# Attention and two MLPs on one core: the reciprocal sums spread over partitions by TensorE instead of through DRAM

## The chip, the cores and the metric

The kernel runs on one core of a Trainium2 chip. The metric is the device time of one execution in microseconds (us). Beside the runs there is one profiled execution, from which every duration here comes. Engines are named as in the profile: PE is TensorE's matmul, PEld its weight load, DVE VectorE, ACT ScalarE, POOL GpSimd, SP SyncE, on whose queue all DMAs are issued.

## The reference

Attention over 4 batches, 8 heads, 576 positions and 64 dimensions a head, in which only scores within tau of the row's maximum count; then two MLPs on the 2304 tokens of width 512.

```python
scores = (q @ k.T) / sqrt(64)
scores = where(scores >= max(scores) - tau, scores, -1e9)
attn = exp(scores - max(scores))
attn = attn / (sum(attn) + 1e-9)
x = (attn @ v)                            # heads side by side: [2304, 512]
h = x @ w_in                              # [2304, 2048]
P = a0 + a1*h + a2*h**2 + a3*h**3
Q = 1 + abs(b0)*abs(h) + abs(b1)*h**2
x = (P / (Q + 1e-6)) @ w_out              # [2304, 512]
out = ((x @ w1) * (x @ w2)) @ w3 @ w_out2 # [2304, 512]
```

## The kernel before

Attention is worked per batch b (4), head pair c (4) and part u: u = 0 takes queries 0 to 255, u = 1 queries 256 to 511 together with the 64 queries that are left, the tail (u = 2 in `pv`), in which both heads of the pair share one block of 128 rows. For each block of 128 queries and each head, `qk` puts 576 scores a row into PSUM (tile S), `top` takes the maximum on DVE, `thr` the threshold, and `exp` the exponentials p and their row sum, one column of a small tile with queries on the partitions. p is split into an f16 part and its remainder (`p_hi`, `p_lo`, tile hl), turned by a DMA transpose (`p_t`, tiles pT and pL), and multiplied with the values, which are split likewise (vh, vl): `pv` makes 28 products of the form 64 head dimensions x queries, alternating between the two heads, whose results take partitions 0 to 63 and 64 to 127 of one PSUM bank (tag h, two banks).

The result has the queries along the columns, while the sums lie one query to a partition. `recip` (lines 551 to 559) adds 1e-9, inverts, transposes the tile in 32 x 32 blocks on DVE (sT) and writes it to DRAM (d_r). `spread` reads it back with each head's row repeated on 64 partitions (tile R). `x_split` and `x_tail` multiply the products in PSUM with R and split the outcome into two f16 parts, the input x of the first MLP (tiles xp, xl).

The MLPs work on 128 tokens (n, 18 of them): `h_product` (line 815), a rational function on ACT, DVE and POOL (tiles U, A, r, gg), a DMA transpose (`turn`, gg into gt), `y_product` (879); then `ab_product` (986), their product, another transpose, and `o_product` (1015). The weights arrive as 64-bit floats, are converted by three integer operations on DVE (`conv_w`, lines 683 to 689), scaled and split into two f16 parts (`split_w`), all in the first third.

Nothing is scheduled at run time. All steps are collected as numbered events; the string ORDER lists them, one token a step, with the letter of the engine for elementwise steps (v DVE, a ACT, p POOL) and the slots of the buffers that it takes. The program issues them in that order, and each engine works through its own part of it in order, waiting on semaphores. Helpers (`copy`, `rest`, `tt`, `small`) issue on the engine of the letter, so one line of theirs (330 to 353) stands for many steps.

Of the kernel before, what the change touches and what calls it, by code (L numbers as in the profile page):

```python
# [36 lines left out]
123a 43.7 16 43 127v.1 125.7 125a 156.1.0 43 16 30.1 140.1 129p 72.0 140 53.1 154p 159.0 161
134v.0 163v.1 136v 165.8 53 32.8 138 167.7 39.9 32 165a 39 167a 77.0.0 32 74.10 62.1 39 53 74
169a.0 59.2 79 171p 53 79p 173.0 74 79p 182.1.0 64.11 81.0 80.0 64 106.1 184.1 186 80 64 188a.2
190.8 61.12 116.1 55v.13 190a 61 175v.5 192.2 61 192a 219.1.0 83v.2.2 99.2 200a.0 207.0 177p 131  # L40
66.1 194p.3 221.2 83 207 202v 76.0 223 66 196v 101.14 198 225v.0 101 227.7 66 101 230.2 227a 209.1
112.2 230a 66 232p.8 142.0 78.15 118.16 78 244.1.0 118 78 118 85.0 80 234v 103.1 246.3 238p.1 80
248 240v 250a.1 252.3 215.4.6 82a.17 87.18 252a 107.0 114.19 87 255.7 114 257a.2 87 107 255a 114
89.0 68v.20 217p 598.2 269.1 70.0 93.1 105.21 269 259v 105 263a.3 283.1.0 281 105 93 91.22 623.1
285.0 287 107 91 288a.2 601.23 91 107 601 618.0 265v 601 290.7 93 626.24 143.2 290v 626 93 626
604.1 95a.25 620.26 620 620 97.1 144.1 128.0 57.0 179.1 146 146v 590.1 146p 242.2 590 130.27
109v.28 271.0 130 590 204 292.5 145.29 606.30 145 130 590 267 145 292v 147.1 148.0 609.0 606 120.2
277.1.0 606 151.1 609 294v.3 296p 609 299v.7 150a.3.3 301p 609 150 135.0 305.1.0 611a.31 122.32
593v.33 279p 596.0 307.1 122 308 122 153.34 166.2 124.0 310v.0 153 314.5 126.0 628.1 153 110.0
137.35 132.0 158.1 137 314a 137 321a.6 174.0 628 168.36 323p 168 312.5 133 628 168 312a 205.2  # L50
139.0 141 628 327.0 631a.37 176.38 160.39 176 160 176 160 189.0 178.0 149 328.2 354 316a.4 181.1
155.1 149 330a.1 206.40 157.1 318v 162.1 206 164 614.1 206 170.1 191.41 197.2 191 172 180 191 180
212.0 193.1 183.42 183 183 199.43 220.1 185.0 199 187.0 199 211.1 214.44 235.2 201.0 214 214 228.0
195 203 222.45 236.0 216.1 213 222 208.0 218.1 213v 210 222 303.1 237.46 224.1 210 213p 634.0 226
237 237 278.1 350.5.8 229.47 239.0 229 84.1 229 636 261 231.1 332.7 233 241 332v 356.1.0 291.2 241
304.0 325 339.0 352a 280.48 243 280 243 339 358.3 247a.49 245v.0 360 334a.2 273.0 272v.50 253a.51
361p.2 268v.52 251a.53 280 424.0 336p 371.1 424 253.0 297.0 275 264p.54 256a.55 249a.56 266a.1 424
274a.0 275a 424 253a 264.1 275v 306.10 260a.12 424 341.1 254a.11 247.0 258v.15 264a 306 363.7
251.1 306 247a 373.14 365.6 284.0 256.0 251v 262a.18 373 319 249.1 270a.21 373 256a 363a 260.0
311.1 249a 365a 378.1.0 286.22 260a 286 372a.3 286 367a.4 266.1 380.0 374p 317.0 381 254.0 266a  # L60
369v 383p.0 385.0 272.1 313.19 370.2 293.16 387.6 313 254a 293 385a 444.1 313 387a 293 331.1 426.0
272a 320.23 324.2 394a.7 320 338.4 320 426 396p 322.1 337.0 274.0 428.0 333.30 258.1 430 274v
400.1 430 270.0 258v 443 401.1 444 270v 403a.1 405.6 326.6 333 262.1 276a.4 326 446.1 333 268.0
446.0 326 351.1 428.1 448 357.2 268a 340.2 428.0 448 262a 347.1.0 433v 405a 340 446.1 412.1 435
340 445.0.1 412 435 349 376.0 353.3 437.0 461.1 353 344.0 414.0 447.2 349p 343.0 349v 461 437 398
345.0 437 345a 508.0 449 345p 463.0 437p 451a.2 466 453.1 508 439.0 353 309.1 359.26 315.1 407v.2
# [1177 lines left out]
```

## Time and profile before

| | us |
|---|---|
| median of 3 runs | 1139.39 |
| lowest and highest | 1138.14, 1145.7 |
| profiled execution, its own time | 1143.35 |
| its span | 1141.6 |
| PE busy in it | 1003.3 |
| DVE busy | 867.7 |
| ACT busy | 594.2 |
| POOL busy | 370.9 |

The span runs from the first instruction to the last of the profiled execution; 1.75 us of its own time lie around it. Busy time counts each engine by itself, so the engines overlap, and a share over the span is a mean over stages that are limited by different things. Mean durations of matmuls include their passage through the array, and neighbours overlap; what one costs in a stream is read from the chain, where a stretch of so many is given with its length.

### The profile page before, as it was taken

The numbers are of one execution on the slowest core, as the hardware profiler recorded it, in microseconds if no ns is written. First come the engines' busy times: TensorE is split into PE (matmuls) and PEld (weight loads), VectorE is DVE, ScalarE is ACT, GpSimd is POOL, SyncE is SP. The second block draws the span as 40 slices with busy tenths as digits, with TensorE's granted clock in tenths as the row PEclk, the third lists the DMA queues.
The fourth block names the chain that finished last, engine by engine and source line by source line (L and its number), as shares of the span: only waits on it lengthen the run. The fifth ranks groups of instructions, "written<-read, shape, count | busy, mean of one in ns | idle before, by whom it ended". The sixth has DMA issues, their size and how long they took to land.

```text
span 1141.6 us, 15703 instructions
## 1 busy us (share of the span) xinstructions
PE 1003.3 (88%) x5284; PEld 475.8 (42%) x5284; DVE 867.7 (76%) x1682; ACT 594.2 (52%) x1086; POOL 370.9 (32%) x377
## 2 busy tenths in 40 slices
PE   2779578388879898989899999899999998999998
PEld 1334233143334443444344444454444444444443
DVE  5886879888876699888798877988787765676552
ACT  4341566775554484747356545767755434352410
POOL 1220121561234234244434343643423322421211
PEclk9999779599999999999899999999999999999999
DMA  7978697766673958778675879795566446723223
GB/s 224 244 211 190 219 210 191 182 112 175 166 175 106 161 109 153 156 139 165 114 136 107 163 139 165 134 152 128 125 130 111 104 85 94 117 53 68 53 56 83
DMA packets 345088, 159.90 MB, mean 140 GB/s; under 512 B 313776, under 2 KB 321968, under 8 KB 345008
## 3 DMA queue, kind: packets, MB, share of 16 engines
q1 hardware_dynamic: 345008, 158.91, 66.7%
q8 instruction: 41, 0.67, 0.3%
q14 instruction: 39, 0.32, 0.1%
HBM read 74.71 MB, written 8.65 MB: 73 GB/s over the span
## 4 chain that ended last, share of the span: by engine, by line
PE 45%; DVE 17%; DMA 10%; issue 4%; ACT 4%; POOL 2%; SPq 2%; DVEq 0%; ACTq 0%; POOLq 0%
PE y L879 9%; PE h L815 9%; PE h L986 6%; PE y L1015 6%; PE S L986 5%; DMA gt<-gg 3%; PE h L601 3%; PE S L504 3%; DVE m L513 2%; DMA pT<-hl 2%; PE y L739 2%; DMA raw<-in_q_dram 2%; DMA R<-d_r 1%; PE S L499 1%; DVE U L835 1%
## 5 line engine op out<-in xcount | busy, mean ns | idle before, releaser
L879 PE MATMUL y<-wp,gt 128*128 128x512 f16 x864 | 200.5, 382 | 9.2 <-DMA gt<-gg 8.1
L815 PE MATMUL h<-wp,xp 128*128 128x512 f16 x768 | 180.4, 383 | 8.5 <-ACT wp L330 2.2
L346 POOL TENSOR_TENSOR hl<-p,hl 128x576 f16<-128x576 f32 x76 | 107.7, 1419 | 167.3 <-ACT hl L330 69.3
L504 PE MATMUL S<-raw 64*128 64x288 f32 x512 | 104.2, 472 | 50.2 <-DVE p L539 20.1
L986 PE MATMUL h<-wp,yy 128*128 128x512 f16 x576 | 137.6, 385 | 6.3 <-DVE U L837 3.1
L879 PEld LDWEIGHTS <-gt 128*128 128x128 f16 x864 | 83.4, 98 | 116.5 <-DMA gt<-gg 11.3
L513 DVE TENSOR_REDUCE m<-S 128x1 f32<-128x576 f32 x144 | 104.3, 748 | 28.0 <-PE S L504 19.5
L815 PEld LDWEIGHTS <-xp 128*128 128x128 f16 x768 | 74.0, 99 | 103.3 <-issue 21.0
L1015 PE MATMUL y<-wp,gt 128*128 128x512 f16 x432 | 103.4, 387 | 7.7 <-DMA gt<-gg 6.6
L346 POOL TENSOR_TENSOR gg<-A,r 128x512 f16<-128x512 f32 x46 | 60.8, 1323 | 137.6 <-DVE A L858 93.2
L536 ACT ACTIVATE S<-S,th 128x576 f32<-128x576 f32 x101 | 70.4, 709 | 63.3 <-DVE th L353 42.8
L823 ACT ACTIVATE U<-h,cf 128x512 f32<-128x512 f32 x72 | 55.8, 776 | 83.9 <-PE h L815 43.2
L986 PEld LDWEIGHTS <-yy 128*128 128x128 f16 x624 | 60.3, 99 | 90.2 <-issue 22.0
L504 PEld LDWEIGHTS S<-raw 64*128 64x128 f32 x512 | 56.7, 204 | 93.8 <-issue 26.1
L346 POOL TENSOR_TENSOR A<-A,r 128x512 f32<-128x512 f32 x41 | 54.1, 1321 | 108.9 <-ACT r L830 102.2
L835 DVE SCALAR_TENSOR_TENSOR U<-h,cf,U 128x512 f32<-128x512 f32 x72 | 53.5, 744 | 42.7 <-ACT r L830 18.9
L541 ACT ACTIVATE p<-S,xy 128x576 f32<-128x576 f32 x101 | 74.7, 742 | 10.4 <-DMA pL<-hl 6.3
L845 ACT ACTIVATE r<-A,lnb 128x512 f32<-128x512 f32 x72 | 52.0, 722 | 45.2 <-POOL A L346 27.1
L854 DVE SCALAR_TENSOR_TENSOR gg<-U,cf,r 128x512 f16<-128x512 f32 x72 | 58.3, 812 | 19.4 <-ACT r L847 16.1
L739 PE MATMUL y<-cw,dg 128*128 128x512 f32 x112 | 62.1, 636 | 11.6 <-DVE wp L334 6.2
L1015 PEld LDWEIGHTS <-gt 128*128 128x128 f16 x432 | 41.9, 100 | 61.2 <-DMA gt<-gg 8.4
L936 PE MATMUL h<-cw 128*128 128x512 f32 x128 | 62.3, 638 | 5.4 <-DVE cw L334 3.6
(195 smaller groups left out, 1672.9 us busy)
## 6 DMA issues: line engine op xcount, KB each, us to landing
rw<-in_moe_w_dram SPq DMA_DIRECT2D x32, 512.0 KB
rw<-in_moe_w_out_dram SPq DMA_DIRECT2D x24, 512.0 KB
raw<-in_k_dram SPq DMA_DIRECT2D x32, 288.0 KB
wr<-in_v_dram SPq DMA_DIRECT2D x16, 576.0 KB
rw<-in_moe_w_in_dram SPq DMA_DIRECT2D x16, 512.0 KB
wr<-in_v_dram SPq DMA_DIRECT2D x16, 320.0 KB
R<-d_r SPq DMA_DIRECT2D x32, 128.0 KB
out_dram<-A SPq DMA_DIRECT2D x16, 256.0 KB
```

What stands on the lines that cost most here:

```text
L346: (nc.gpsimd if eng[0] == "p" else nc.vector).tensor_tensor(o, x, y, op=op)
L504: nc.tensor.matmul(t[s][:, half, :HS], x[r, o:o + 128], y[r, keys], start=True, stop=True)
L513: nc.vector.tensor_reduce(st["m", b, c, blk][:, s:s + 1], t[:, :, :HS], axis=AX.XY, op=ALU.max, negate=True)
L536: nc.scalar.activation(t, t, AF.Prelu, bias=th, alpha=BIG)
L541: nc.scalar.activation(x, t, AF.Exp, bias=xy[:, 0:1], accum_out=su)
L739: nc.tensor.matmul(y, st["dg", dg], r, start=True, stop=False)
L815: nc.tensor.matmul(t, x[:, y, c, o:o + 128], w[:, a, :], start=c + i == 0, stop=c == KD - 1 and i == 2)
L835: stt(u, h, cf[:, 4:5], u, ALU.mult, ALU.mult)
L879: nc.tensor.matmul(st["y", n], x[:, 4 * a + j, :], w[:, y, :], start=f + j + i == 0, stop=f == 3 and j == 3 and i == 2)
L936: nc.tensor.matmul(t, st["cw", ("w3", m, j // 4)][:, o:o + 128], st["cw", ("wo2", j)], start=j == 0, stop=j == 7)
L986: nc.tensor.matmul(t, x[:, 4 * y + c, :], w[:, a, :], start=c + i == 0, stop=c == KD - 1 and i == 2)
L1015: nc.tensor.matmul(st["o", n], x[:, 4 * a + j, :], w[:, y, :], start=hf + j + i == 0, stop=hf == 1 and j == 3 and i == 2)
```

## The change

The reciprocal sums no longer go through DRAM. `recip` writes each reciprocal, times 1024, as an f16 value and an f16 remainder (tile rr). `spread` multiplies on PE: the stationary operand is one column of rr repeated 64 times, the moving one a diagonal tile (spot) with 2^-10 on it, so that column q of the result holds the reciprocal of query q on all 64 partitions; value and remainder add up in PSUM. It uses the upper half of the h bank whose lower half then takes `pv`'s products, and its second step copies the result into R on ACT or DVE. A full spread is 8 products, a tail spread (u = 2, which is now a step of its own) 4. The sums lie in tiles of five columns from a pool of three. ORDER is a new table for the new list of events: its tokens are renumbered, and steps change their places and, for 551 steps, their engine.

```diff
 ORDER = """
...
@@ -305,7 +308,7 @@
     BUFS = dict(
         w=57, gg=2, gt=3, xp=2, x4=4, dg=2, wr=3, U=2, A=2, r=2, G=9, pT=3, vh=4, vl=4,
-        R=2, m=4, th=3, sT=2, vs=2, sc=4, cf=6, xl=1,
+        R=2, m=4, th=3, su=3, rr=3, vs=2, sc=4, cf=6, xl=1,
     )
     places = []
@@ -363,7 +366,6 @@
         events.append((fn, args, *stream))
-    d_r = [dr.tile([32 * 128], F32, name=f"d_r{j}") for j in range(2 * B * NP)]
     d_y = [dr.tile([128, 1024], F16, name=f"d_y{n}") for n in range(NT)]
@@ -380,7 +382,7 @@
     lnb = cst.tile([128, 1], F32, name="lnb")
     c3 = cst.tile([128, 3], F32, name="c3")
     onesh = cst.tile([128, 128], BF16, name="onesh")
-    sums = [cst.tile([128, 32], F32, name=f"sums{j}") for j in range(3)]
+    spot = cst.tile([128, 128], F16, name="spot")
     qp = cst.tile([128, 128], F32, name="qp")
     wsc = cst.tile([128, 8], F32, name="wsc")
     acc = cst.tile([128, 56], F32, name="acc")
@@ -396,8 +398,9 @@
         nc.sync.dma_start(out=bb, in_=cb.rearrange("(o c) -> o c", o=1).to_broadcast([128, 2]))
         nc.gpsimd.memset(unit, 1.0)
         nc.gpsimd.memset(onesh, 1.0)
-        for t in sums:
-            nc.gpsimd.memset(t, 0.0)
+        nc.gpsimd.memset(spot, 0.0)
+        nc.gpsimd.affine_select(out=spot, in_=spot, compare_op=ALU.not_equal, fill=2.0**-10,
+                                base=0, pattern=[[-1, 128]], channel_multiplier=1)
         nc.vector.tensor_scalar(flag, tau_t, 0.0, 0.125, op0=ALU.is_ge, op1=ALU.mult)
@@ -525,9 +528,9 @@
         u = min(blk // 2, 1)
         if (u, s) == (0, 0) and blk == 0 or (blk, s) == (2, 0):
-            st["su", b, c, u] = sums[(2 * (NP * b + c) + u) % 3]
+            st["su", b, c, u] = T("su", [128, 5])
         p = T("G", [128, S], name="p")
-        x, k = p.rearrange("p (j c) -> p j c", j=2), 2 * s + blk - 2 * u if blk < 4 else 4
+        x, k = p.rearrange("p (j c) -> p j c", j=2), 2 * (blk - 2 * u) + s
         su, th = st["su", b, c, u][:, k:k + 1], st["th", b, c, blk][:, s:s + 1]
         t, m = st["S", b, c, blk][s][:, :, :HS], st["m", b, c, blk][:, s:s + 1]
         if by_dve(b, c, blk):
@@ -550,23 +553,30 @@
     def recip(b, c, u):
         n = 5 if u else 4
-        su, d = st["su", b, c, u], d_r[2 * (NP * b + c) + u]
-        nc.vector.tensor_scalar(su[:, :n], su[:, :n], 1e-9, None, op0=ALU.add)
-        nc.vector.reciprocal(su[:, :n], su[:, :n])
-        t = T("sT", [128, 32])
-        nc.vector.transpose(t, su)
-        yield
-        nc.sync.dma_start(out=d.rearrange("(k i q) -> i k q", i=4, q=32), in_=t)
+        su = st.pop(("su", b, c, u))[:, :n]
+        nc.vector.tensor_scalar(su, su, 1e-9, None, op0=ALU.add)
+        nc.vector.reciprocal(su, su)
+        t = st["rr", b, c, u] = T("rr", [128, 2, 5], F16)
+        nc.vector.tensor_scalar(t[:, 0, :n], su, 1024.0, None, op0=ALU.mult)
+        stt(t[:, 1, :n], su, 1024.0, t[:, 0, :n], ALU.mult, ALU.subtract)
     def spread(b, c, u):
-        d = d_r[2 * (NP * b + c) + u]
-        r = st["R", b, c, u] = T("R", [128, 320])
-        t = d[0:512].rearrange("(h o q) -> h o q", h=2, o=1)
-        nc.sync.dma_start(out=r[:, 0:256], in_=t.to_broadcast([2, 64, 256]))
-        if u:
-            t = d[512:640].rearrange("(h o q) -> h o q", h=2, o=1)
-            nc.sync.dma_start(out=r[:, 256:320], in_=t.to_broadcast([2, 64, 64]))
+        t, r = P("h", [128, 512]), st["rr", b, c, min(u, 1)]
+        st["pv", b, c, u] = t
+        for i in range(2 if u < 2 else 1):
+            for a in range(2):
+                for h in range(2):
+                    o, k = slice(64 * h, 64 * h + 64), slice(0, 128)
+                    w, d = r[:, a, 2 * i + h:2 * i + h + 1], t[o, 256 + 128 * i:384 + 128 * i]
+                    if u == 2:
+                        k, w, d = o, r[o, a, 4:5], t[o, 64:128]
+                    nc.tensor.matmul(d, w.to_broadcast([k.stop - k.start, 64]), spot[k, k],
+                                     start=a == 0, stop=a == 1)
+        yield
+        n = 256 if u < 2 else 64
+        y = st["R", b, c, u] = T("R", [128, n])
+        copy(y, t[:, n:2 * n])
     def p_hi(b, c, blk, s):
         hl = T("G", [128, 2 * S], F16, name="hl")
@@ -591,7 +601,7 @@
         n = 256 if u < 2 else 64
         if u < 2 and c == 0:
             st["xp", b, u] = T("xp", [128, 2, KD, TG], F16)
-        t = P("h", [128, 512])
+        t = st["pv", b, c, u]
         vh, vl = st["v", b, c]
         for j in range(14):
             for s in range(2):
@@ -603,12 +613,10 @@
                                  start=j == 0, stop=j == 13)
         for s in range(2 if u < 2 else 1):
             st.pop(("pT", b, c, u, s))
-        st["pv", b, c, u] = t
     def x_split(b, c, u):
-        t, r = st.pop(("pv", b, c, u)), st["R", b, c, u]
-        y, p = r[:, :256], st["xp", b, u]
+        t, y, p = st.pop(("pv", b, c, u)), st.pop(("R", b, c, u)), st["xp", b, u]
         nc.vector.tensor_tensor(y, t[:, :256], y, op=ALU.mult)
         yield
         copy(p[:, 0, c, :], y)
@@ -619,10 +627,10 @@
     def x_tail(b, c):
-        t, r = st.pop(("pv", b, c, 2)), st["R", b, c, 1]
+        t, y = st.pop(("pv", b, c, 2)), st.pop(("R", b, c, 2))
         if b % 2 == 0 and c == 0:
             st["xl", b // 2] = T("xl", [128, 2, KD, 128], F16)
-        y, p = r[:, 256:320], st["xl", b // 2][:, :, c, 64 * (b % 2):64 * (b % 2) + 64]
+        p = st["xl", b // 2][:, :, c, 64 * (b % 2):64 * (b % 2) + 64]
         nc.vector.tensor_tensor(y, t[:, :64], y, op=ALU.mult)
         yield
         copy(p[:, 0], y)
@@ -648,10 +656,11 @@
                 at(p_lo, b, c, blk, s)
                 at(p_t, b, c, blk, s)
         at(recip, b, c, u)
-        at(spread, b, c, u)
         if u:
+            at(spread, b, c, 2)
             at(pv, b, c, 2)
             at(x_tail, b, c)
+        at(spread, b, c, u)
         at(pv, b, c, u)
         at(x_split, b, c, u)
```

The order table is not legible as such; the rows that follow are each engine's instructions in program order. First SP at the last head pair of the last batch (b = 3, c = 3, u = 1): before,

```order
L586 DMA_TRANSPOSE pT<-hl 128x9x128 x4
L867 DMA_TRANSPOSE gt<-gg 128x8x128
L559 DMA d_r_97<-sT 4x32x32
L586 DMA_TRANSPOSE pT<-hl 128x9x128
L586 DMA_TRANSPOSE pL<-hl 128x9x128
L566 DMA R<-d_r_97 128x1x256
L569 DMA R<-d_r_97 128x1x64
L586 DMA_TRANSPOSE pL<-hl 128x9x128
L867 DMA_TRANSPOSE gt<-gg 128x8x128 x2
```

and with the change, at the same place:

```order
L596 DMA_TRANSPOSE pT<-hl 128x9x128
L1036 DMA out_dram<-A 128x512
L596 DMA_TRANSPOSE pT<-hl 128x9x128 x2
L596 DMA_TRANSPOSE pL<-hl 128x9x128
L596 DMA_TRANSPOSE pT<-hl 128x9x128 x3
L596 DMA_TRANSPOSE pL<-hl 128x9x128
L876 DMA_TRANSPOSE gt<-gg 128x8x128 x4
```

The write of sT to d_r and the two reads into R are gone from between the transposes of P (pT, pL) and of the MLP's tiles (gt); 80 such DMAs go in all.

Next DVE at the same head pair, where the last row sum is finished (the accumulation of p) and inverted: before,

```order
L539 SCALAR_TENSOR_TENSOR p,sums_129<-S,th,p 128x576
L554 TENSOR_SCALAR sums_129<-sums_129 128x5
L555 RECIPROCAL sums_129<-sums_129 128x5
L557 STREAM_TRANSPOSE sT<-sums_129 128x32
L334 CAST hl<-p 128x576
L334 CAST xl<-R 128x64
L346 TENSOR_TENSOR xp<-R,xp 128x256
```

and with the change:

```order
L542 SCALAR_TENSOR_TENSOR p,su<-S,th,p 128x576
L557 TENSOR_SCALAR su<-su 128x5
L558 RECIPROCAL su<-su 128x5
L560 TENSOR_SCALAR rr<-su 128x5
L561 SCALAR_TENSOR_TENSOR rr<-su,rr 128x5
L337 CAST xp<-R 128x256
L863 SCALAR_TENSOR_TENSOR gg<-U,cf,r 128x512
L349 TENSOR_TENSOR hl<-p,hl 128x576
L863 SCALAR_TENSOR_TENSOR gg<-U,cf,r 128x512
L337 COPY R<-h 128x256
```

Two small operations on rr stand where the transpose was, and a copy of the spread values from the h bank into R follows four rows later, ahead of the multiplication.

Last PE at the same head pair with the change, where the spread stands (its eight pairs of weight load and product; the first is shown):

```order
L888 LDWEIGHTS gt
L888 MATMUL y<-wp,gt 128x512
L574 LDWEIGHTS rr
L574 MATMUL h<-spot,rr 64x128
...
L888 LDWEIGHTS gt
L888 MATMUL y<-wp,gt 128x512
...
L995 LDWEIGHTS x_9292
L995 MATMUL S<-wp,x_9292 128x512
L611 LDWEIGHTS vh
L611 MATMUL h<-pT,vh 64x256
```

Here 24 products of the MLPs (lines 888 and 995, which are 879 and 986 before) stand between the spread and the products with P (line 611, before 601). In 35 of the 48 cases nothing stands between them.

## Rows read from the trace of the kernel before

**Rows 1.** The profile page, first part: busy time (share of the span) and instructions

```profile
span 1141.6 us, 15703 instructions
PE 1003.3 (88%) x5284; PEld 475.8 (42%) x5284; DVE 867.7 (76%) x1682; ACT 594.2 (52%) x1086; POOL 370.9 (32%) x377
```

**Rows 2.** Windows: stretch, length; busy us by engine (count); granted clock, DMA share, GB/s

```profile
0.00:300.00 300.00, 212.48 (x802) 98.41 (x802) 240.49 (x499) 161.55 (x317) 78.07 (x87) 0.90 0.77 192
300.00:1000.00 700.00, 654.09 (x3803) 315.79 (x3803) 549.07 (x1047) 385.59 (x694) 266.61 (x267) 0.98 0.70 134
```

**Rows 3.** The chain that ended last: shares by engine (page); by line (query)

```profile
PE 45%; DVE 17%; DMA 10%; issue 4%; ACT 4%; POOL 2%; SPq 2%; DVEq 0%; ACTq 0%; POOLq 0%
by line: PE y L879 9.5%; PE h L815 9.4%; PE h L986 6.4%; PE y L1015 6.2%; PE S L986 4.8%; issue 3.7%; DMA gt<-gg 3.2%; PE h L601 2.6%; PE S L504 2.6%; DVE m L513 2.1%; DMA pT<-hl 1.8%; PE y L739 1.6%; DMA raw<-in_q_dram 1.5%; DMA R<-d_r 1.5
```

**Rows 4.** Waits of PE up to 300 us: waiter <- awaited: us, times, longest

```profile
PE S L504 <- DVE p L539: 17.8, 3, 10.7
PE S L504 <- DVE raw L336: 12.3, 1, 12.3
PE y L739 <- DVE wp L334: 6.2, 6, 2.3
```

**Rows 5.** Waits of PE from 300 to 1000 us, same columns

```profile
PE y L879 <- DMA gt<-gg: 8.1, 5, 2.1
PE y L1015 <- DMA gt<-gg: 6.6, 4, 3.2
```

**Rows 6.** The chain in order of time, two stretches: start us, us, what

```profile
802.38 1.65 PE h L601 x28
804.03 1.40 PE h L986 x6
809.30 1.29 PE h L986 x6
981.76 2.09 PE h L601 x56
992.68 5.50 DMA R<-d_r
```

**Rows 7.** Timeline of PE: start us, us, instructions, idle before and its releaser

```profile
998.77 4.05 PE L815 MATMUL h<-wp,xp 128*128 128x512 f16 x18 [1.64 <-DVE R L612]
```

**Rows 8.** Who waited for tile R: us, times

```profile
  PE h L815: 2.5, 3
```

**Rows 9.** Instruction groups by form: count, busy us, mean ns, idle before

```profile
L601 PE MATMUL h<-pL,vh 128*64 128x64 f16 x288 | 7.6, 199 | 0.0
L554 DVE TENSOR_SCALAR sums<-sums 128x5 f32<-128x5 f32 x16 | 8.1, 505 | 2.2 <-ACT p L541 1.9
L554 DVE TENSOR_SCALAR sums<-sums 128x4 f32<-128x4 f32 x16 | 3.8, 240 | 8.1 <-ACT p L541 7.9
L557 DVE STREAM_TRANSPOSE sT<-sums 128x32 f32<-128x32 f32 x32 | 6.8, 212 | 1.1
L612 DVE TENSOR_TENSOR R<-h,R 128x256 f32<-128x256 f32 x32 | 13.4, 419 | 11.0 <-PE h L601 9.2 <-DMA R<-d_r 1.6
L346 DVE TENSOR_TENSOR gg<-A,r 128x512 f16<-128x512 f32 x26 | 19.2, 740 | 0.3
L346 POOL TENSOR_TENSOR gg<-A,r 128x512 f16<-128x512 f32 x46 | 60.8, 1323 | 137.6 <-DVE A L858 93.2 <-issue 17.4 <-ACT S L536 16.5
L336 DVE TENSOR_SCALAR vh<-wr,vs 128x1152 f16<-128x1152 f32 x3 | 5.2, 1720 | 0.0
```

**Rows 10.** DMA issues of the round trip: count, issue ns min/median/max, first and last

```profile
L559 SPq DMA_DIRECT2D d_r<-sT x32: 544/597/1393, 29.9 to 989.1; - x32
L566 SPq DMA_DIRECT2D R<-d_r x32: 500/528/582, 37.2 to 992.7; - x32
L569 SPq DMA_DIRECT2D R<-d_r x16: 489/504/1682, 163.4 to 993.2; - x16
```

**Rows 11.** Weight conversions on DVE: ns min/median/max, first and last start

```profile
L689 DVE SCALAR_TENSOR_TENSOR cw<-rw,cw x72: 647/685/1765, 10.7 to 339.4; 128x512 int32<-128x512 int32 x72
```

More of the change, by code (lines that the diff above doesn't have):

```diff
@@ L37 @@
[L37 to L66, printed above, removed]
@@ new lines @@
+1149.1 998.0.1 1039a 1151 1034p 1096 1391 1039p 998 1152v.0 1001a 1006 1382 1025.0 1154.5 1673
+1395v.1 1382 1025 1001 1053.1 1116.0 1025 1384a.1 1003.0 1117 1053 1116a.1 1025p 1154v 1384 1393.1
+1119 1191v.1.1 1119a 1393 1308v.3.3 1009 1191 1033.0 1308 1120.0 1397 1579.2 1033 1119v 1671.2
+1504.3 1397p.1 1504 1111.1 1167.0 1397p 1035.0 1111v.0 1504 1035.0 1112 1400.0 1035.1 1114 1168.3
+1404.1 1114a 1122a.2.2 1041p 1038 1027.2 1170v.2 1404 1038 1172.4 1122 1043 1054.0 1124.6.0
+1138v.2 1157a.1 1172v 1043 1568.0 1156.7 1054 1140v 1156v 1141.2 1030.0 1173v.8 1057.1 1046.1
@@ new lines @@
+1518p 1477.1 1921.1 1523.0 1477.0 1525 1487p 1519.0 1482p 1480 1917.1 1527a.1 1528.5 1480 1484
+1917 1451.1 1530.6 1528v 1484 1919.0 1342.3.0 1530v 1451 1921 1342 1451 1344a 1590.0.1 1532v.1
+1344 1451p 1919 1349 1347.2 1592.2 1581.0 1937 1437.0 1534v 1453.0 1923a.0 1538v.5 1926 1539p
+1488.0 1490.1 1854.2 1594 1351 1596v.2 1486.0 1541 1597.1.6 1506.1 1487v 1486 1597v 1506 1514.2
+1926v.1 1486 1543.0 1926v 1509.1 1486v 1437 1509.0 1934.0 1545.3 1588 1509.1 1577.1 1547v.0 1455
+1511 1513p 1489.2 1599.2 1583 1511 1548.5 1455 1599v 1659.1 1515 1601p.7 1536 1548a 1473 1603p
@@ new lines @@
+1736 1661a.3.3 1950 1765.1 1805.3 1959p 1807 1736a 1624.0 1598 1736p 1961.1 1598 1809p.2 1801v
+1661 1624 1810.1.8 1586 1783v.4 1810a 1600.1 1738.1 1812.7 1785v 1626.1 1814v.5 1787 1738 1600
+1626.0 1816v 1626.1 2156.2 1963 1812a 1600 1818.0 1631v 1740.0 1963 1629 1600p 1633 1742 1633
+1825.0.1 1602.2 1629 1742 1642.0 1635.0 1827.1 1642 1635 1829 1604.0 1635 1831p.0 1834.8 1604
+1635v 1832.4 1778p.6 1638.1 1834a 1622 1779v 1832a 1841v.0 1781 1820v.5 1644.1 1862.1.0 1847.0
+1843p 1644.1 1789.1 1622 1644.0 1863.0 1740.0 1649p 1646 1740.1 1640 1865 1836a.3 1651 1646 1640
@@ new lines @@
+1838v 1651 1867v.1 2163.1 1840 1653.1 1869.2.8 1744v 1871.6 2163 1653 1858.4.3 1746 1821v 1869a
+2161.0 1653 1746 1871a 1653v 2161 1749.0 1655.2 1749 1883.1.0 2166a.1 1749 1860a 1790.0 2168 1749p
+1792.0 1790v.0 1885.2 1751.0 1887 1791.1 2168p.1 1794 1889a.2 1891.7 1794p 1791 2168p 1891v
+1872v.1 1893.2 2171.1 1755.0 1893v 1874v 1755 1905.2 1876.2 1894a.8 1794v 1916.1.0 1896v 1758.0
+1823.1 1793.1 1658 1760 1793.1 1918.3 1793.0 1658 1920 1898 1965a.0 1797p 1760 1753.1 1795
+1660.2.0 1965 1845 1922v.0 1800 1795 1753 1924.1.7 1660 1800 2176.1 1662a 1666 2197 1802.1 1925.1
@@ new lines @@
+2324a.1 2106.0.1 2324p 2311 2108.2 2110 2025.0 2026 2325.1 2025v.0 2063 2111v.2 2028 2113.1.1
+2002v.4 2028v 2003v 2101.8.2 2327.0 2066.1 2028v 2113v 2066.0 2005 2327 2066.0 2068 2071p 2030
+2068 2103p 2073 2050 2073 2076.0 2315a.1 2050 2115.4 2315v 2329v.0 2316.0 2084.1 2115v 2076
+2126.0.1 2076 2328.0 2128.1 2076p 2129 2317 2085v.7 2131v.0 2087v 2317 2069v.5 2070p 2084 2134.6
+2328 2134a 2146.1 2330 2029.0 2330p.1 2147.3 2133.3 2031.1 2169 2029v.1 2330p 2133a 2429.0 2149p.1
+2331.2 2033 2033p 2033p 2429 2052.2 2125.0 2078.0 2431a.1 2430 2072 2151.0 2430 2151v 2157.1
```

425 lines of the change are left out of this document (214 added, 211 removed).

## Prediction

> **What bounds the kernel now.** I read the page's first part first: TensorE (PE) is busy for 1003.3 of 1141.6 us, VectorE (DVE) for 867.7, ScalarE for 594.2, GpSimd (POOL) for 370.9 [rows 1]. A share over the whole span hides stages, so the windows come next. Up to 300 us PE is busy for 212.48 us and idle for 87.5, while DVE is busy for 240.49 and the DMA engines for 77%. From 300 to 1000 us PE is busy for 654.09 of 700 us, 93%, and DVE for 549.07, 78% [rows 2]. So there are two regimes: a front in which weights are converted and attention starts, with slack on PE and little on DVE, and a long rest in which PE is nearly full. The chain that ended last agrees: PE has 45% of it, DVE 17%, DMA 10%, and the broadcast read that the change removes has 1.5%, which is 17.1 us of the span [rows 3].
>
> What PE waits for differs as well. In the front, the three longest waits for DVE make 36.3 of the 87.5 idle us [rows 4]. In the rest, transposes of the MLP's tiles (gg into gt) are the largest named wait, 8.1 + 6.6 = 14.7 us [rows 5]. Tile R, the spread reciprocals, held PE up for 2.5 us in three places, through DVE's multiplication [rows 8].
>
> **PE: 320 small products are added.** There are 32 full spreads (two per head pair and batch) of eight products with 128 moving columns, and 16 tail spreads of four products with 64. The nearest rows are the products with P. Twenty-eight with 256 columns take 1.65 us, 59 ns each; in the stretch where 28 with 64 columns follow directly, the 56 take 2.09 us, so the latter cost 0.44 us, 15.7 ns each [rows 6]. Going by columns, 128 lies a third of the way: 30 ns. That gives 32 x 8 x 30 ns = 7.7 us and 16 x 4 x 15.7 ns = 1.0 us, together 8.7. The bounds are 15.7 ns for all 320 (5.0 us) and 59 ns for the 256 larger ones (16.1 us).
>
> The array is also used in halves there, and going back costs something: the first six MLP products behind products with P take 1.40 us, and six in mid-stream 1.29, so 0.11 us [rows 6]. In the new order 35 of the 48 spreads stand directly ahead of their product with P, 13 apart from it; the 16 tail spreads use quarters of the array where their products use halves. I count 29 extra changes at 0.11, 3.2 us (bounds: none, or twice that). PE's addition is then 11.9 us.
>
> A quarter of it (batch 0) falls into the front, where 87.5 us of idle time cover it at no cost; that cover would go only if the front became bound by PE. Three quarters, 8.9 us, fall where PE is busy for 93% of the time and on the chain for 45%: between 4.0 and 8.3 us reach the end. I take the middle, **+6.2 us**, because nothing says which of the gaps the added work can use. With the bounds of the prices the term reaches from 5.0 x 0.75 x 0.45 = 1.7 to 22.5 x 0.75 x 0.93 = 15.7 us.
>
> The trace and a page part here. With the row's 59 ns for 256 columns, 30 ns for 128 follows. The Trainium skill, "TensorE: Matmul & The Clock Gate", section "Back-to-back issue gap", gives about 81 ns per product with 128 columns in a stream of weight loads and products; by it the 256 products would cost 20.7 us and the sum would rise by some 7 us. The trace disagrees, since its products with twice the columns already run below that.
>
> **DVE: more work, part of it in the front.** A reciprocal loses its 32x32 transpose (32 x 0.212 = 6.8 us) and gains two small instructions, a scaled cast and a remainder. I price the cast like the existing addition on four or five columns (16 x 0.505 + 16 x 0.240 = 11.9 us) and the remainder like the four-column one (7.7). Of the copies of the spread values out of PSUM, DVE has 22, at most 0.419 each: 9.2 us. The new order also moves 13 of the remainders gg<-A,r from POOL, where one takes 1.323 us, to DVE at 0.740: 9.6 us [rows 9]. That makes 31.6 us more on DVE; other moves among the engines about cancel on DVE and relieve POOL. Since POOL and ScalarE have 2% and 4% of the chain [rows 3], I cost their changes at nothing.
>
> What counts is where DVE's addition lies. Weight conversions end at 339.4 us [rows 11]. DVE's rows ahead of the last of them, each at its group's mean, add up to 303 us before and 319 with the change, 16 more; the largest piece is three more scalings of a value tile at 1.720 [rows 9]. It lies in the stage in which PE waits for DVE in 36.3 of its 87.5 idle us [rows 4], 41%, so I take 0.41 x 16 = **+6.6 us** (bounds 0 and 16). DVE's other half comes where DVE has 22% of slack, and I cost it at nothing; without that slack it would be the next thing that is late.
>
> **The round trip that goes.** One transpose result is written to DRAM and read back. At the last head pair the read alone has 5.50 us of the chain [rows 6], and DVE's product with R and PE behind it wait; yet PE's idle time there is 1.64 us [rows 7], 30% of it. Applied to all 17.1 us that reads have on the chain this is **-5.1 us**. The bounds are the 2.5 us that PE was seen to wait [rows 8] and the whole 17.1. What is late next, where the read goes, is the transpose of P and PE's own queue.
>
> SyncE issues 80 DMAs fewer (32 + 32 + 16, about half a microsecond each [rows 10]) out of the 567 of the program, and no longer stands in front of the MLP's transposes waiting for a reciprocal or for the write. PE's 14.7 us of waits for such transposes [rows 5] are the bound on that side. I take the share of the DMAs that go, 14%: **-2.1 us**.
>
> What the change adds as a wait: a spread stands in PE's queue and needs the two small DVE results and a free h bank, and the bank is held from the spread until the multiplication. In the new order 4 to some 390 steps lie between reciprocal and spread, so I cost the first at nothing; the bank is mostly held only 0.2 to 0.3 us longer. The multiplication waits for the copy instead of the read; the copy runs beside the 1.65 us of products with P.
>
> **Sum.** 6.2 + 6.6 - 5.1 - 2.1 = +5.6 us. The profiled execution took 1143.35 us and would become 1149.0; it is 4 us above the median of the runs shown, 1139.39, on which I put the same difference: **1145 us**.
>
> **Rivals.** About 1% (11.4 us) is what a measurement of this kernel tells from no change, so I divide there.
>
> (a) Forecast: a small loss or none, within 1%: chance 0.44.
>
> (b) Faster. The round trip was a link of the chain, not just late in one place. Then all 17.1 us go, with the 2.1 of SyncE; DVE's addition hides under the DMA engines' 77% in the front [rows 2], and PE's costs 8.9 x 0.45 = 4.0. Sum -15.2, 1124 us. For it: PE's order was free to change, and the read's 5.50 us is long beside a PE stretch. Against it: PE's direct waits for R are 2.5 us [rows 8]. Chance 0.23.
>
> (c) Slower, through DVE in the front. If DVE is what the front waits for, all 16 us arrive at 339.4 us, and the full PE behind cannot give them back. With PE's 6.2, and only 2.5 and 2.1 us returned, the sum is +17.6, 1157 us. It decides from 9.8 of the 16 us. For it: DVE at 80% busy in the front, the weight scalings that move to it. Against it: 51 of the 87.5 idle us of PE do not end on those waits for DVE. Chance 0.27.
>
> (d) Slower, through changes of array shape. If each of the 29 extra changes lets the array run empty at both ends, at the mean of a lone small product, 0.199 us [rows 9], they cost 11.5 us instead of 3.2; PE's term becomes 20.2 x 0.75 x 0.93 = 14.1 and the sum +13.5, 1153 us. The Trainium skill, "TensorEngine Tiling (Array Packing)", section "Key Properties", says that a change of tiling mode drains the engine, without a price. By the row such a change costs 0.11 us; by that rule alone it could be the dearer one. Chance 0.06.
>
> **Range and chances.** The unknowns add up to 1.7 + 0 - 17.1 - 14.7 = -30 us and 15.7 + 16 - 2.5 - 0 = +29 us if all fall to one side. To hold the time 8 times in 10 I take about four fifths of that around the cases above: 1121 to 1164 us; the forecast's own range is 1128 to 1151. Faster 0.23, within 1% 0.44, slower 0.27 + 0.06 = 0.33.
>
> **What would show it.** PE's new line: 320 products, some 30 ns each on the chain (an uninterrupted full spread near 0.24 us, a tail near 0.06); PE's busy time near 1015 us. DVE's busy time near 899 us, with the last weight conversion 6 us later, near 346. No R<-d_r on the chain, and waits for gt near 12.6 us. If PE's idle time up to 300 us falls below 80 us, (b) is gaining; if it exceeds 95, (c). If spreads stretch to half a microsecond or more, or six products behind them take 1.6 us, (d). The prediction is wrong if the new order packs PE's middle stage (300 to 1000 us) more or less tightly by itself: each percent of its 93% is 7 us, as much as any term above.

## The result and the profile after

| | before | after |
|---|---|---|
| median, us | 1140.72 (4 runs) | 1106.93 (4 runs) |
| lowest and highest | 1138.14, 1145.7 | 1105.37, 1107.28 |
| profiled execution, its span | 1143.35, 1141.6 | 1106.88, 1105.1 |

The changed kernel takes 0.970 of the time before, with an interval of 0.9665 to 0.9735. It is faster by 34 us, where 6 us slower was forecast, and 14 us below the range. The prediction was wrong in sign and in size.

The profile page of the kernel after, first part (busy time, share of the span, instructions), and its line on the DMA queue:

```profile
span 1105.1 us, 16168 instructions
PE 997.3 (90%) x5599; PEld 480.3 (43%) x5604; DVE 869.7 (79%) x1756; ACT 599.9 (54%) x1118; POOL 330.9 (30%) x350
q1 hardware_dynamic: 334544, 153.67, 61.6%
```

After, windows: stretch, length, busy us by engine (count), granted clock, DMA share, GB/s:

```profile
0.00:300.00 300.00, 216.54 (x862) 101.71 (x867) 253.60 (x534) 157.18 (x315) 69.98 (x85) 0.89 0.72 193
300.00:1000.00 700.00, 681.23 (x4223) 333.45 (x4223) 567.02 (x1134) 412.81 (x754) 242.95 (x247) 1.00 0.63 129
```

Beside [rows 1, 2] this says where the time came from. In the front PE's idle time goes from 87.5 to 83.5 us. From 300 to 1000 us it goes from 45.9 to 18.8, and that is most of the gain. The mean granted clock there rises from 0.98 to 1.00. The clock's records show why: between 300 and 1000 us the kernel before has six stretches at 1.2 GHz, together 27 us, and the rest at 2.4 GHz; after has none. (Both fall again at the very end.) The DMA share falls from 0.70 to 0.63. PE is busy for 6 us less in the whole span although it has 320 products more. A window holds more work in the faster kernel, so of the windows idle times are compared, not busy times.

What PE waits for, after, from 300 to 1000 us (waiter <- awaited: us, times, longest): the two largest, and all for transposes.

```profile
PE h L824 <- DVE U L846: 2.9, 2, 2.4
PE h L574 <- ACT r L839: 2.0, 2, 1.7
PE y L888 <- DMA gt<-gg: 1.1, 2, 0.8
PE y L1024 <- DMA gt<-gg: 0.8, 1, 0.8
```

The waits for the MLP's transposes, 14.7 us in [rows 5], are 1.9. The chain says the same. After, it can be followed back only to 741 us; from there to 1000 us it has two DMAs:

```profile
746.59 4.48 DMA gt<-gg
911.89 3.35 DMA pT<-hl
```

In the kernel before the chain has five DMAs in that stretch, 25.9 us, four of them transposes gt<-gg and the fifth the read of R in [rows 6]. So what left the kernel is lateness of DMAs, and of the MLP's transposes above all, which the change does not touch. The experiments ask how a trip of 80 small DMAs made them late.

### The profile page after: what moved, and what is told of

It reads as the page before. It is cut to its first block, busy times and chain, and to the rows that moved or that the text cites. A ratio compares the mean times of both kernels' runs of the same rounds, so it can differ in the third digit from the quotient of the medians.

```text
span 1105.1 us, 16168 instructions
## 1 busy us (share of the span) xinstructions
PE 997.3 (90%) x5599; PEld 480.3 (43%) x5604; DVE 869.7 (79%) x1756; ACT 599.9 (54%) x1118; POOL 330.9 (30%) x350
## 5 line engine op out<-in xcount | busy, mean ns | idle before, releaser
L888 PE MATMUL y<-wp,gt 128*128 128x512 f16 x864 | 198.6, 379 | 1.7 <-DMA gt<-gg 1.1
L507 PE MATMUL S<-raw 64*128 64x288 f32 x512 | 96.9, 458 | 47.8 <-ACT p L544 25.9
L995 PE MATMUL h<-wp,yy 128*128 128x512 f16 x576 | 132.6, 379 | 5.3 <-DVE R L634 1.9
L516 DVE TENSOR_REDUCE m<-S 128x1 f32<-128x576 f32 x144 | 104.4, 750 | 19.6 <-PE S L507 15.9
L1024 PE MATMUL y<-wp,gt 128*128 128x512 f16 x432 | 99.7, 379 | 0.8 <-DMA gt<-gg 0.8
L539 ACT ACTIVATE S<-S,th 128x576 f32<-128x576 f32 x97 | 67.7, 710 | 53.4 <-POOL th L356 33.7
L507 PEld LDWEIGHTS S<-raw 64*128 64x128 f32 x512 | 53.8, 198 | 88.1 <-ACT p L544 33.9
L349 POOL TENSOR_TENSOR gg<-A,r 128x512 f16<-128x512 f32 x33 | 46.3, 1403 | 111.1 <-DVE A L867 76.8
L863 DVE SCALAR_TENSOR_TENSOR gg<-U,cf,r 128x512 f16<-128x512 f32 x72 | 59.1, 824 | 22.6 <-ACT r L856 15.6
L544 ACT ACTIVATE p<-S,xy 128x576 f32<-128x576 f32 x97 | 71.6, 742 | 6.3 <-POOL hl L349 3.5
```

Source lines behind the costliest of these rows:

```text
L349: (nc.gpsimd if eng[0] == "p" else nc.vector).tensor_tensor(o, x, y, op=op)
L507: nc.tensor.matmul(t[s][:, half, :HS], x[r, o:o + 128], y[r, keys], start=True, stop=True)
L516: nc.vector.tensor_reduce(st["m", b, c, blk][:, s:s + 1], t[:, :, :HS], axis=AX.XY, op=ALU.max, negate=True)
L539: nc.scalar.activation(t, t, AF.Prelu, bias=th, alpha=BIG)
L544: nc.scalar.activation(x, t, AF.Exp, bias=xy[:, 0:1], accum_out=su)
L863: stt(p[:, 0, :], u, cf[:, 3:4], r, ALU.add, ALU.mult)
```

## The experiments

Times are medians, each with the kernel before on the same chip (1140.5 to 1142.4 us); ratios are to that.

| kernel | us | ratio, interval |
|---|---|---|
| E1 new order, trip through DRAM | 1147.90 | 1.0066 (1.0032 to 1.0100) |
| E2 old order, spread on PE | 1125.72 | 0.9878 (0.9844 to 0.9912) |
| E4 old order, no trip, no spread | 1095.44 | 0.9605 (0.9575 to 0.9635) |
| E5 old order, trip's DMAs, unused | 1140.43 | 0.9995 (0.9973 to 1.0017) |
| E11 as E5, writes alone | 1095.58 | 0.9604 (0.9566 to 0.9641) |
| E8 old order, reads cut per head | 1107.29 | 0.9697 (0.9655 to 0.9739) |
| E9 new order, reads cut per head | 1106.01 | 0.9688 (0.9643 to 0.9733) |
| E12 old order, reads cut along queries | 1147.54 | 1.0061 (1.0035 to 1.0086) |
| E13 as E9, reads issued by ScalarE | 1102.29 | 0.9666 (0.9646 to 0.9686) |
| E14 as E8, reads issued by ScalarE | 1108.30 | 0.9729 (0.9701 to 0.9756) |
| E7 after, without spread and copies | 1088.22 | 0.9536 (0.9496 to 0.9576) |

**The two halves of the change apart: E1 and E2.** E1 keeps the table of the new order and does the trip as before: the write four steps behind the reciprocal, the reads at least 17 behind it. The tail's read goes into a tile of its own. (Lines left out are marked by three dots, here and below.)

```diff
+        nc.vector.transpose(t, su)
+        yield
+        nc.sync.dma_start(out=d.rearrange("(k i q) -> i k q", i=4, q=32), in_=t)
...
+        nc.sync.dma_start(out=r, in_=t.to_broadcast([2, 64, 256]))
+        if u:
+            r = st["R", b, c, 2] = T("Rt", [128, 64])
...
+            nc.sync.dma_start(out=r, in_=t.to_broadcast([2, 64, 64]))
```

> The new order table with the old way of spreading: the sums go through DRAM again, the write four steps behind the reciprocal, the read 17 steps behind it or 45 steps ahead of the product with P, whichever is later; no spreads on PE. Theory A (the round trip itself held the old kernel back, by late data or by its place in SyncE's queue): most of the gain goes, 1130 to 1150 us. Theory B (the new order packs PE more tightly by itself, and the way of spreading matters little): 1100 to 1115 us, near the changed kernel's 1107.

Measured 1147.9 us: the new order with the old trip gains nothing. In its waits of PE from 300 to 1000 us the transposes are back, and more of them:

```profile
PE y L875 <- DMA gt<-gg: 17.0, 8, 4.2
PE y L1011 <- DMA gt<-gg: 5.4, 5, 2.2
PE h L597 <- DMA pT<-hl: 5.3, 2, 5.1
PE h L597 <- DMA pL<-hl: 5.0, 2, 3.3
```

E2 is the reverse: the order before, with each spread directly ahead of its products with P and the copy three steps later, on ACT and DVE in turn.

```diff
-        nc.sync.dma_start(out=d.rearrange("(k i q) -> i k q", i=4, q=32), in_=t)
+        nc.vector.tensor_scalar(t[:, 0, :n], su, 1024.0, None, op0=ALU.mult)
+        stt(t[:, 1, :n], su, 1024.0, t[:, 0, :n], ALU.mult, ALU.subtract)
...
+                    nc.tensor.matmul(d, w.to_broadcast([k.stop - k.start, 64]), spot[k, k],
+                                     start=a == 0, stop=a == 1)
```

> The old order table with the new way of spreading: each spread stands directly ahead of its product with P, its copy three steps later, in turn on ScalarE and VectorE; the 80 DMAs are gone. Theory A: most of the gain comes, 1105 to 1120 us. Theory B: no gain, the work added to PE shows, 1140 to 1155 us.

Measured 1125.72 us: a part of the gain, and outside both ranges. The new order alone gives nothing, and taking the trip away gives something without it. Whether the new order adds the rest can't be told from E2, whose placing of spreads and copies was not tuned.

**Late data or the DMAs themselves: E4 and E5.** Both keep the order before and multiply by a constant in place of the reciprocals, so nothing waits for the trip. E4 leaves its 80 DMAs out. E5 issues them, the reads into a tile that nobody uses. The lines shown are E5's; E4 has no R2.

```diff
+        places.clear()
+        r = T("R2", [128, 320])
...
-        nc.vector.tensor_tensor(y, t[:, :256], y, op=ALU.mult)
+        nc.vector.tensor_scalar(y, t[:, :256], 2.0**-8, None, op0=ALU.mult)
```

> The kernel before, its order untouched, without the 80 DMAs of the round trip; the products with P are multiplied with a constant, so the division by the sums is left out. Theory A: this is the most that taking the trip away can give in the old order, 1100 to 1120 us. Theory B: 1130 to 1140 us, since the trip was hidden.

> As the run without the trip, but the write and the reads are still issued at their old places, into a tile that nothing uses; the division is left out. It splits theory A: if the late data cost the time, it is as fast as the run without the trip, 1100 to 1120 us; if the DMAs' place in SyncE's queue did, it stays at 1135 to 1145 us. Theory B: like the kernel before, 1135 to 1142 us.

Measured 1095.44 us, 5 us below its range, and 1140.43 us: 45.0 us lie between them. The theory of late data falls, since E5 needs no value of the trip and is as slow as the kernel before. The windows from 300 to 1000 us of E4, and then of E5, show PE and the DMA share:

```profile
300.00:1000.00 700.00, 680.30 (x3953) 329.94 (x3953) 574.87 (x1078) 401.75 (x722) 275.57 (x273) 1.00 0.61 129
```

```profile
300.00:1000.00 700.00, 653.96 (x3821) 316.11 (x3823) 555.76 (x1061) 391.20 (x703) 266.17 (x268) 0.99 0.72 135
```

E4 has the numbers of after, E5 those of before. The unused DMAs take a tenth of the DMA engines' time and move hardly more a second.

**Which DMAs: E11.** E5 without its 48 reads; the 32 writes stay.

```diff
-        r = T("R2", [128, 320])
-        nc.sync.dma_start(out=r[:, 0:256], in_=t.to_broadcast([2, 64, 256]))
-        if u:
...
-            nc.sync.dma_start(out=r[:, 256:320], in_=t.to_broadcast([2, 64, 64]))
```

> Kernel before with a constant in place of the reciprocals, the 32 writes of the trip left in and its 48 reads left out (nothing uses what is written). With all 80 DMAs left in this takes 1140.4 us, without any 1095.4. Few-engines theory: the reads are the cost, 1094 to 1103 us. SyncE theory: SyncE still waits for every reciprocal ahead of the transposes queued behind the write, so 1110 to 1135 us.

Measured 1095.58 us, the same as without any of the trip. The writes, and SyncE's wait for every reciprocal in front of its transposes, cost nothing. The reads, with SyncE's wait for the write ahead of each, cost all 45 us. E8 below keeps these waits.

**What a read does.** One instance in the kernel before, first SyncE's timeline (start, length of the issue, DMA), then the chain, then PE's timeline (idle time and its releaser in brackets):

```profile
865.25 0.52 SPq L566 DMA_DIRECT2D R<-d_r  x1
865.82 0.49 SPq L569 DMA_DIRECT2D R<-d_r  x1
866.41 3.98 SPq L867 DMA_TRANSPOSE gt<-gg  x1
```

```profile
866.41 6.05 DMA gt<-gg
```

```profile
872.51 1.47 PE L879 MATMUL y<-wp,gt 128*128 128x512 f16 x6 [1.57 <-DMA gt<-gg]
```

The reads themselves are issued in half a microsecond each. The transpose behind them holds SyncE for 3.98 us, lands after 6.05, and PE waits 1.57 us for it. A transpose's issue has a median of 1.30 us in this trace. Of the 22 that stand directly behind a read, 11 take 3.98 to 5.26 us, and all 11 have a full read and a tail's in front. Behind a lone full read the first transpose takes 1.24 to 2.33 us, and in five of eight cases it is the next one that takes 2.94 to 3.46. Other stretches read alike, for instance these two, with SyncE held for 4.30 and 4.06 us:

```profile
537.63 0.52 SPq L569 DMA_DIRECT2D R<-d_r  x1
538.26 4.30 SPq L867 DMA_TRANSPOSE gt<-gg  x1
...
670.60 0.51 SPq L569 DMA_DIRECT2D R<-d_r  x1
671.20 4.06 SPq L867 DMA_TRANSPOSE gt<-gg  x1
```

The packets' records in the traces say more. A full read is 128 packets of 1024 bytes, a tail's read 128 of 256. In the kernel before, 27 of the 32 full reads stand apart from other packets of their size. They take 3.49 us from first to last (median), and their durations add up to 2.0 times that: on average two of the 16 DMA engines work on them, if each has one packet at a time (the records do not name the engine). The transposes' packets also have 256 bytes. The median of that size is 18 ns, but 376 packets last over 2 us, in 21 groups of 13 to 21; in 20 of the groups packets of 1024 bytes pass meanwhile. At the instance above, 19 packets that start from 868.9 us on last 2.06 to 2.30 us. No other packet of 256 bytes starts from 869.2 to 870.1, and all 19 end at 871.2, after the full read (867.1 to 870.1) and the tail's behind it. So it is not only those packets that share an engine with the read: for a while all transposes stand still. Why two engines can hold up all of them the records do not show.

The read's source is written as two heads, 64 copies each, 256 values, so its outermost dimension is 2. The Trainium skill, "DMA: Bandwidth & Descriptors", section "Rules for kernel authors", says that a transfer whose outermost dimension is smaller than 16 is confined to at most that many engines; the traces agree, with 2.0.

**Is it the two engines: E8 and its control E12.** E8 cuts each read into one per head. Bytes, packets and order stay; 48 DMAs more are issued, and the outermost dimension of each becomes the 64 copies. The tail's reads are cut likewise.

```diff
-        nc.sync.dma_start(out=r[:, 0:256], in_=t.to_broadcast([2, 64, 256]))
+        for h in range(2):
+            nc.sync.dma_start(out=r[64 * h:64 * h + 64, 0:256],
+                              in_=d[0 + 256 * h:256 + 256 * h].rearrange("(o q) -> o q", o=1)
+                              .to_broadcast([64, 256]))
...
```

> Kernel before, its order unchanged; only each broadcast read of the reciprocals is cut into two reads, one per head: 64 partitions that all read the same row, in place of one transfer whose outermost dimension is the 2 heads. Bytes and packets stay the same, SyncE issues 48 DMAs more. Few-engines theory: in the records of before, the read's 1024-byte packets pass on about two of the 16 DMA engines for 3 to 4 us, and the transposes' packets queued there wait behind them (376 packets longer than 2 us); spread over 16 engines the wait is gone, and most of the 45 us between the kernel before and the one without the trip return: 1095 to 1112 us, fewer than 100 packets over 2 us. SyncE theory (issuing and waiting for the trip's DMAs holds the transposes back): 48 more issues at about 0.5 us, 1140 to 1160 us. Data theory (total bytes and packets): no change, 1135 to 1147 us.

E12 cuts the same reads along the queries: as many DMAs as E8, with the two heads still outermost. Its packets have half the size and are twice as many.

```diff
-        nc.sync.dma_start(out=r[:, 0:256], in_=t.to_broadcast([2, 64, 256]))
+        for a in (0, 128):
+            nc.sync.dma_start(out=r[:, a:a + 128], in_=t[:, :, a:a + 128].to_broadcast([2, 64, 128]))
...
```

> Control for the halved reads: kernel before, its order unchanged, each broadcast read again cut into two reads, so that SyncE issues the same 48 DMAs more, but cut along the queries: each half still has the 2 heads as its outermost dimension. Few-engines theory: nothing is gained, since each half still passes on the same few engines (the packets have half the size and are twice as many): 1135 to 1165 us, over 250 transposes' packets longer than 2 us. If cutting a transfer in two is by itself what helped (shorter transfers, finer interleaving with the transposes): 1100 to 1115 us as with the cut along the heads.

Measured 1107.29 and 1147.54 us. SyncE's timeline and the chain in E8, at the instance shown above:

```profile
833.05 1.76 SPq L566 DMA_DIRECT2D R<-d_r  x2
834.86 1.23 SPq L571 DMA_DIRECT2D R<-d_r  x2
836.19 1.25 SPq L871 DMA_TRANSPOSE gt<-gg  x1
```

```profile
836.19 3.25 DMA gt<-gg
```

The same transpose is issued in 1.25 us and lands after 3.25. The 22 transposes directly behind a read have a median of 1.31 us, and none takes over 1.40. In E12:

```profile
871.18 1.07 SPq L567 DMA_DIRECT2D R<-d_r  x2
872.31 2.80 SPq L571 DMA_DIRECT2D R<-d_r  x2
875.21 1.96 SPq L870 DMA_TRANSPOSE gt<-gg  x1
```

```profile
875.21 3.92 DMA gt<-gg
```

Here the tail's reads are held up themselves, and the transpose after them. The 22 such transposes take 1.92 to 3.26 us. The table sets the traces side by side; its last column is how long SyncE's issues of all transposes and of all reads of R last together.

| kernel | a full read, first to last packet, us | engines on it | 256-byte packets: mean ns, over 2 us | SyncE's issues, us |
|---|---|---|---|---|
| before | 3.49 | 2.0 | 26.4, 376 | 460.5 |
| E5 | 3.56 | 2.0 | 26.7, 373 | 460.0 |
| E12 | 3.52 | 2.0 | 24.4, 139 | 483.7 |
| E8 | 1.48 | 4.5 | 23.0, 38 | 432.0 |
| E11 (no reads) | | | 22.6, 17 | 381.8 |
| after (no reads) | | | 22.9, 17 | 381.7 |

In E8 and E12 a full read is both its halves; E8's 4.5 is a mean over two transfers with the gap between their issues. The number of DMAs is thus not the cost, nor their bytes: E8 and E12 issue the same number and move the same bytes, and 40 us lie between them. Nor are the packets, since E8 has those of the kernel before and is 34 us faster. One expectation for E12 failed: 139 packets over 2 us, not over 250. Why they are fewer is not shown. E12 has 361 packets between 1 and 2 us, but the kernel after, which has no reads, has 354. The time agrees with the theory of few engines, and SyncE's issues go the way of the times. No run varied the number of engines beyond these two cases.

E8 also answers what the change was needed for. Cutting the reads, eight lines in place of four, gives the old kernel the changed kernel's time, 1107.29 against 1106.93.

**The same in the new order: E9.** E1 with its reads cut per head.

> The new order with the trip through DRAM put back (1147.9 us), its reads cut in two in the same way. Few-engines theory: all that the trip cost there goes, 1085 to 1110 us, at or below the changed kernel's 1106.9, since TensorE's spread products and the copies are absent. SyncE theory: 1145 to 1165 us. If the new order is by itself worse than the old one, it stays above the old order with halved reads.

Measured 1106.01 us, 42 below E1. With two-engine reads the new order is no better than the old (E1 against before), with halved ones neither (E9 against E8).

**What the spread costs: E7.** The changed kernel without the 320 products and the 48 copies; a constant takes the place of the spread values.

```diff
-                    nc.tensor.matmul(d, w.to_broadcast([k.stop - k.start, 64]), spot[k, k],
-                                     start=a == 0, stop=a == 1)
...
-        copy(y, t[:, n:2 * n])
```

> The changed kernel, order unchanged, without the 320 spread products and without the 48 copies of their sums (a constant takes the place of the spread reciprocals; the two-part reciprocals are still computed). My price for the products was 6.2 us at the end: 1097 to 1102 us. If they cost what they cost in the old order (1125.7 with them, 1095.4 without trip or spread, 30 us): 1075 to 1085 us. If they are hidden in the new order: 1104 to 1108 us.

Measured 1088.22 us, in none of the three ranges: products and copies cost 18.7 us of the changed kernel, above my price and below the 30 of the old order (E2 less E4). Why the old order pays 12 us more was not tried further; E2's placing of the spreads and copies is mine, not a tuned one.

**What halved reads still cost: E13 and E14.** E9 and E8 with the reads issued by ScalarE.

```diff
-            nc.sync.dma_start(out=r[64 * h:64 * h + 64, 0:256],
+            nc.scalar.dma_start(out=r[64 * h:64 * h + 64, 0:256],
```

> The new order with the trip and its reads halved per head (1106.0 us), the 96 reads issued by ScalarE in place of SyncE. What separates it from 1088.2 us (no trip, no spread) is either SyncE's queue, in which the reads and their wait for the write stand in front of transposes: then 1090 to 1102 us, which would beat both kernels; or the reads' packets and late data: 1104 to 1110 us. If ScalarE, which waits in order for each write to land, is held up by it: 1110 to 1130 us.

> The kernel before with the halved reads (1107.3 us), issued by ScalarE. Against 1095.6 us with the writes alone, the same three cases: SyncE's queue, 1097 to 1104 us; packets and late data, 1105 to 1110 us; ScalarE held up by the wait for the write, 1110 to 1135 us.

Measured 1102.29 us, just above the range for SyncE's queue, and 1108.30 us. In the old order this takes off nothing; in the new one it takes off 4 us by the medians, but the intervals of the ratios overlap (0.9688 and 0.9666). Yet PE's waits for transposes from 300 to 1000 us are only 3.0 us in E13:

```profile
PE y L879 <- DMA gt<-gg: 3.0, 4, 1.3
```

In E9 they are, in the same view:

```profile
PE y L879 <- DMA gt<-gg: 5.9, 6, 1.5
PE h L601 <- DMA pT<-hl: 5.0, 2, 3.7
PE y L1015 <- DMA gt<-gg: 3.1, 4, 1.0
PE h L601 <- DMA pL<-hl: 2.3, 1, 2.3
```

So a part of what halved reads cost in the new order may be their place in SyncE's queue; the times do not prove it. E13 is the fastest complete version here, 0.9666 (0.9646 to 0.9686) beside the changed kernel's 0.970 (0.9665 to 0.9735): at best slightly faster, and the intervals overlap. What the rest of the 12 us in the old order (E8 less E11) and of the 14 in the new one (E13 less E7) is, packets, late data or waits for the write, stays open. Whole reads issued by ScalarE were not run either. So it is open whether a whole read holds the transposes up because it shares SyncE's queue with them, or on the DMA engines whatever the queue.

## Why the prediction was wrong

By differences of these runs the change has three parts: the new order with the old trip, +7 us (E1); the trip's going, -59.7 us in the new order (E1 to E7) and -45.0 in the old one (E5 to E4); the spread and its copies, +18.7 us (E7 to after). The forecast's sum was -7.2 for the trip and +12.8 for what is added.

**The step that failed: the round trip that goes, with both of its terms.** It was priced at -7.2 us and measured -45.0 and -59.7. The -5.1 us were a share of the 17.1 that R's reads have on the chain, bounded by that 17.1 and by PE's 2.5 us of waits for R [rows 3, 8]. That prices the trip by those who wait for its data, and E5 shows that this was not what cost the time: nothing waits for the data there, and the time stays at 1140.43 us. The -2.1 for SyncE's queue priced the trip by its share of the number of DMAs, 14%, with issues of half a microsecond [rows 10]. These rows were right and beside the point: the read is issued quickly, and the DMA behind it pays. I had [rows 5] as a bound, but did not ask why a transpose was late. SyncE's timeline of the kernel before held the answer, 3.98 us for an issue whose median is 1.30. All 270 transposes together hold SyncE for 434.9 us in E5 and for 381.8 in E11. I do not claim that these 53 us are the 45 lost, since not each transpose is waited for.

**The bounds** fell for the same reason. -17.1 and -14.7 were taken from what the chain and PE's waits name last. Even all of their sum, -30 us, stops short of the -34 measured, although 18.7 us of added work stand against it. A queue that is late throughout shows in the last waits only in part. One other part is the clock: 27 us at the lower of its two levels are worth up to half of that, 14 us. At each of the six falls PE was standing still or just had been, for 1.7 to 5.2 us, but only two of these stops were waits for a transpose gt<-gg. The rest no view here names one by one. (A slip beside this: four fifths of the +29 above 1145 would end at 1168 us, not at 1164.)

**PE's addition** was sized well as work, by other parts than I thought, but not in what of it reaches the end. The chain of the kernel after, in order of time (start, us, what):

```profile
814.85 0.34 PE h L574 x8
815.20 1.53 PE h L611 x28
816.72 2.70 PE h L995 x12
...
889.50 0.18 PE h L574 x4
889.68 0.56 PE h L611 x28
890.24 1.40 PE h L824 x6
...
926.13 0.34 PE h L574 x8
...
929.17 1.65 PE h L611 x28
```

A full spread takes 0.34 us, not 0.24, a tail's 0.18, not 0.06. But the 28 products directly behind a full spread take 1.53 instead of 1.65 [rows 6], together 1.87, 0.22 more than before. Where MLP products stand between, as at 929.17, they take 1.65 again. So it looks as if the spread pays for the change of the array's shape. A lone tail's products take 0.56 in the chain before, too:

```profile
912.36 0.56 PE h L601 x28
```

Of the 32 full spreads 22 stand directly ahead of their products, so 22 x 0.22 + 10 x 0.34 + 16 x 0.18 = 11.1 us, against the 11.9 that I priced. In E7 PE is busy for 985.9 us, 11.4 less than in the kernel after. But of the 11.9 only 6.2 us were to reach the end, at most 15.7 with the bounds, and the time that E7 saves is 18.7: this term was too small, and some 7 us of it are not PE's work. The six products after a tail take 1.40, as before, not 1.6: rival (d) falls. The rule on drains in the Trainium skill, "TensorEngine Tiling (Array Packing)", section "Key Properties", is not contradicted, since the 0.34 us may hold such drains; but 0.22 or 0.34 us is all that a full spread comes to with them.

**The copy** was costed at nothing, as running beside the products with P. It does not where the spread stands directly ahead of them. Timeline after:

```profile
944.88 0.71 PE L611 MATMUL h<-pT,vl 128*64 128x256 f16 x10
945.66 0.42 DVE L337 COPY R<-h 128x256 f32<-128x256 f32 x1 [1.15 <-PE h L611]
946.49 0.42 DVE L620 TENSOR_TENSOR R<-h,R 128x256 f32<-128x256 f32 x1
```

It starts when they end, at 945.6, and the multiplication stands behind it. Some of the 18.7 us of E7, the 7 that are not PE's work above all, may lie here; the runs do not part products from copies.

**DVE in the front** did not lose time. The last weight conversions, and three of the groups on which the term rested:

```profile
L698 DVE SCALAR_TENSOR_TENSOR cw<-rw,cw x72: 676/686/1761, 8.6 to 329.5; 128x512 int32<-128x512 int32 x72
L339 DVE TENSOR_SCALAR vh<-wr,vs 128x1152 f16<-128x1152 f32 x6 | 4.8, 814 | 1.6 <-DMA wr<-in_v_dram 1.6
L349 DVE TENSOR_TENSOR gg<-A,r 128x512 f16<-128x512 f32 x39 | 27.1, 696 | 0.3
L337 DVE COPY R<-h 128x256 f32<-128x256 f32 x16 | 6.8, 423 | 11.8 <-PE h L611 11.7
```

The last of them starts at 329.5 us, 10 earlier than in [rows 11], where 6 later was said. The largest piece, three more scalings of a value tile at 1.720 us, cost nothing: six of them now take 4.8 us, where three took 5.2 [rows 9]. The mean of three was no price. DVE's total rises by 2.0 us, not 31.6. The new instructions came out near my count, 17.7 us for the two parts of the reciprocals (19.6 said), 8.1 for copies (9.2) and 7.9 for the remainders from POOL (9.6), but the other moves did not cancel: they took work off DVE. Rival (c) falls, and PE's idle time up to 300 us, 83.5, lies between the marks of 80 and 95 that were to speak for (b) or (c). DVE is in fact busy for 13.1 us more up to 300 us, but so it is in E4 (255.36 us), which has no spread: more of the work gets done by then. [rows 4] gives waits for DVE alone; the largest of that stretch in the kernel before is for ACT:

```profile
PE h L705 <- ACT sq L696: 19.5, 11, 4.8
```

**Rival (b)** had the sign and its reason, that the trip is a link, in part: it took the trip's data for the link and stopped at 17.1 us. Its cause is refuted by E5, and its 1124 us are 17 too many.

## What to carry to other kernels

Price a DMA by what stands behind it in its queue, not only by who waits for its data: compare the issue times of the same kind of DMA behind it and elsewhere. Before a small broadcast transfer is replaced by compute, look at its outermost dimension; here a cut along the right dimension was worth as much as the whole change, and a cut along the other one nothing. The last waits that a chain names can be far below what a queue that is late everywhere costs: here 17.1 and 14.7 us were named, and 45 were lost.

## What was not expected of the hardware

A read of 128 KB that keeps some two DMA engines busy for 3.5 us held all transposes up: 48 reads, 16 of them the tails', with values that nothing used, cost 45 us (E5 to E11). While that goes on the DMA engines look busy, 0.72 of their time at 135 GB/s in E5 against 0.61 at 129 in E4. A packet that stands still counts as busy: from 300 to 1000 us E5 has 303 packets of 256 bytes that last over 2 us, 854 us together, which is 0.08 of the 16 engines' time in that stretch; E4 has none. So a high DMA share was no sign of work done.
